# One fused attention and MLP kernel: the list that orders its last part is rewritten

## The chip, the core and the metric

The kernel runs on one core of a Trainium2 chip. The core has a matrix engine (PE, with its weight loads shown apart as PEld), a vector engine (DVE), a scalar engine (ACT), GpSimd (POOL) and a queue engine (SP). Each works through its own instructions in the order in which they were written, and they meet at semaphores. The metric is the device time of one execution in microseconds; the median over runs is given.

## The reference

Eight batches with eight heads of 576 tokens attend inside a window of 32 tokens on each side and to eight global tokens. The result, 4608 tokens by 512, goes through an MLP whose activation is h·cos(h):

```python
x = attn_out.transpose(0, 2, 1, 3).reshape(B * S, H * D)      # 4608 x 512
h = x @ w_in                                                  # 512 -> 2048
g = h * np.cos(h)
return (g @ w_out).astype(np.float32)                         # 2048 -> 512
```

## The kernel before

The kernel works in fp16 with fp32 sums. Attention goes by pairs of heads, and the MLP goes by tiles of 512 tokens, nine tiles numbered 0 to 8. The two are interleaved: strings of short words, one word for a step, are read from left to right, and each step writes its instructions. The schedule is manual, so the order of the words is the order of the instructions on every engine. The last string, `TAIL`, starts when all attention is done and 112 of the 144 MLP units in front of the activation are written. It finishes tiles 6, 7 and 8, and it is what the change edits. Its words:

- `i` is one unit in front of the activation (`one`, then `mlp_in` and `mlp_act`): four matmuls of 128x512 into one PSUM bank (L788), a sine on ACT that gives the cosine (L794, "cos") and a product on DVE (L795, "g"). The units of a tile are numbered 0, 8, 1, 9, ... 7, 15. I write i8.15 for unit 15 of tile 8. Banks alternate: two banks named `ph` and two in the tile `units`.
- `o` is one unit behind the activation (`two`, then `mlp_out` and `win`): eight matmuls of 128x256 (L852). Tiles 6 to 8 use Winograd's seven products of half matrices, in the order 1, 2, 6, 5, 7, 3, 4, each in two units for two column halves. I write o8.6a and o8.6b for the two halves of product 6 of tile 8. The banks are `wx` (products 1, 6, 7, 4 added up) and `wy` (2; then 5 and 3). After the products a copy on ACT (L866, L868, L870, L875) or an addition on DVE (L879) takes the bank out, and SP stores the result. In tile 8 this happens for each half by itself, in tiles 6 and 7 once for both.
- `a0` to `a7`, `b0` to `b7`, `c0` to `c7` are the sums of quarters of g that Winograd's products of tiles 6, 7 and 8 need (`g_sum`, L822, DVE, 128x1024). Words 0 to 3 are the first half of the rows, 4 to 7 the second: s1, then s2 from s1, then s4 from s2, and a difference written in place in g. Product 5 reads s1, product 6 s2, product 3 s4 and product 7 the difference.
- `x0`, `x1` are sums of squares of the last attention rows (`x_squares`, L910, ACT).
- `w` squares one of 16 blocks of w_in (`weight_squares`, L923, ACT); from the second of four on, DVE adds it (L925, "wsq"). `v0` to `v3` sum four such blocks over the partitions with one matmul (`weight_norms`, L930, bank `pn`) and take the maximum on DVE (L931).
- `F` is the final check's chain of small DVE instructions (`finish_check`, L937 to L954). `R` is its matmul with one column and the flag (`raise_flag`, L960 to L963).

An `i` of tile 8 may stand only behind the last `o` of tile 6, and an `o` of tile 7 only behind the last `i` of tile 7.

```python
        for step in TAIL.split():
            n = int(step[1:] or 0)
            if step[0] == "i":
                one()
            elif step[0] == "o":
                two()
            elif step[0] == "x":
                x_squares(B * NP // 2 - 1, n)
            ...
            elif step[0] == "v":
                weight_norms(n)
```

Of the kernel before, what the change touches and what calls it, by code (L numbers as in the profile page):

```python
# [48 lines left out]

LASTR = "2 kz qz sa 2 2 2 sz pa 1 j0 2 1 2 xa n pz 1 1 j1 2 xz 1 j2 1 2 1 j3 1"  # L50

TAIL = "i x0 a4 o i x1 a5 o i a6 o i a7 o i w o i w i w o i w o i b0 o i b1 v0 o i b2 i b3 o i w o i w o i w o i w o i b4 o i b5 v1 o i b6 o i b7 o i w o i w i w o i w o i c0 o i c1 v2 o i c2 i c3 o i w o i w o i w o i w c4 c5 c6 c7 v3 o o o o o F o o o o o R o o o o o"

MID = ("+ 1 1 1 1 Z0 1 1 1 Z5 B5 1 Z1 1 1 Z2 1 1 A0 1 Z3 1 1 A1 1 n0 A2 g10 g11 1 Z4 N K6 1 1 1 1 1 1 1 2 2 kc qc n1 2 2 1 1 B6 2 2 n2 kd qd - 2 2")

# [156 lines left out]
def kernel(  # L212
# [787 lines left out]
    with tc.manual_schedule():  # L1000
# [136 lines left out]
        units2 = ps.tile([P, 2, TT], FP32, tag="pv", bufs=1, name="units2")  # L1137
        for step in TAIL.split():
            n = int(step[1:] or 0)
# [54 lines left out]
```

## Time and profile before

| | |
|---|---|
| median of three runs | 339.95 us (339.12, 339.95, 344.02) |
| the profiled execution's own time | 340.63 us |
| its span | 338.9 us, of which PE 322.2 busy (95%) |
| DVE, ACT, POOL busy | 269.4, 241.3, 107.2 us |
| granted TensorE clock over the span | 0.997 |
| the part written by `TAIL`, on PE | 264.3 to 332.1 us |

PE's matmuls overlap, so a row's duration is longer than the distance at which units follow each other; distances between starts are what counts. A row of the timeline with "x8" is eight instructions in a row. The number in square brackets is the idle time of the engine before the row, with what ended it. The end of a matmul in the trace is modelled.

### The profile page before, as it was taken

What the parts mean: (1) busy time and instruction counts of PE and PEld (TensorE: products, weight loads), DVE (VectorE), ACT (ScalarE), POOL (GpSimd) and SP (SyncE); (2) the same over time, 40 slices, a digit from 0 to 9 for tenths busy, and PEclk for the clock granted to TensorE, in tenths of its full rate; (3) what the DMA queues carried; (4) which work ended last, traced back from release to release, by engine and by line L of the source; (5) the groups of instructions that cost most, each with busy time, mean ns of one, the idle gap of its engine ahead of it and who ended that gap; (6) DMA issues with size and microseconds to landing.
All of it is one profiled execution on the core that took longest, in us unless ns stands there. A gap on an engine that the chain in (4) does not pass through costs nothing.

```text
span 338.9 us, 8639 instructions
## 1 busy us (share of the span) xinstructions
PE 322.2 (95%) x3269; PEld 179.8 (53%) x3269; DVE 269.4 (79%) x649; ACT 241.3 (71%) x422; POOL 107.2 (32%) x216
## 2 busy tenths in 40 slices
PE   7989889999999999999999999999999999999791
PEld 3566654444545454545454545454544566666581
DVE  6578989984678798989898988888989778778850
ACT  4778885785968878787878787878786775665510
POOL 7856658451162316232532344143001100000000
PEclk9999999999999999999999999999999999999998
DMA  5999799999999999999999999999970010100212
GB/s 76 203 185 205 140 207 206 196 123 176 131 201 123 155 151 150 219 150 175 160 160 162 160 178 137 163 171 172 124 130 3 31 33 31 64 32 2 93 54 80
DMA packets 167220, 45.01 MB, mean 133 GB/s; under 512 B 153108, under 2 KB 163732, under 8 KB 166996
## 3 DMA queue, kind: packets, MB, share of 16 engines
q1 hardware_dynamic: 107556, 26.73, 54.5%
q0 software_dynamic: 59472, 17.54, 50.6%
q8 instruction: 27, 0.44, 0.6%
q14 instruction: 21, 0.17, 0.2%
q10 hardware_dynamic: 144, 0.13, 0.1%
HBM read 44.93 MB, written 19.17 MB: 189 GB/s over the span
## 4 chain that ended last, share of the span: by engine, by line
PE 82%; DVE 7%; ACT 6%; issue 2%; DMA 1%; SPq 0%; ACTq 0%; DVEq 0%
PE ph L788 29%; PE po L892 23%; PE wx L852 6%; PE wy L852 5%; PE units L788 4%; PE st L722 3%; PE pv L742 3%; DVE g L795 2%; PE tx L767 2%; PE pv L669 2%; PE bank L618 1%; DMA gidx_col<-in_global_idx_dram 1%; ACT cos L794 1%; PE st L654 1%; ACT e L661 1%
## 5 line engine op out<-in xcount | busy, mean ns | idle before, releaser
L788 PE MATMUL ph<-xT,w_in 128*128 128x512 f16 x512 | 123.2, 379 | 1.0 <-DVE g L795 0.4
L794 ACT ACTIVATE cos<-ph,pio 128x512 f16<-128x512 f32 x128 | 86.5, 687 | 44.8 <-PE ph L788 42.2
L795 DVE TENSOR_TENSOR g<-cos,ph 128x512 f16<-128x512 f16 x128 | 85.6, 684 | 18.8 <-ACT cos L794 16.8
L892 PE MATMUL po<-w_out,g 128*128 128x512 f16 x384 | 93.4, 379 | 0.0
L788 PEld LDWEIGHTS <-w_in 128*128 128x128 f16 x576 | 53.7, 98 | 57.4 <-issue 1.4
L892 PEld LDWEIGHTS <-g 128*128 128x128 f16 x384 | 36.5, 98 | 43.1
L725 ACT ACTIVATE e<-st 128x512 f16<-128x512 f32 x44 | 23.9, 594 | 8.2 <-PE st L722 8.1
L726 DVE TENSOR_TENSOR pm<-e,mask 128x512 f16<-128x512 f16 x44 | 18.8, 428 | 13.4 <-ACT e L725 12.1
L1079 POOL COPY gate<-xn 1x1 f16<-1x1 f16 x8 | 1.4, 180 | 81.0 <-DVE xn L753 81.0
L775 POOL COPY xT<-xg 128x4 f16 x48 | 15.8, 330 | 32.0 <-DVE xT L770 29.4
L281 POOL DMA_DIRECT2D q<-in_q_dram x11 | 24.3, 2205 | 0.0
L852 PEld LDWEIGHTS <-g 128*128 128x128 f16 x192 | 18.7, 98 | 5.7 <-issue 0.3
L753 DVE TENSOR_TENSOR xn<-pv,r_all 128x768 f16<-128x768 f32 x22 | 21.1, 958 | 0.7
L914 ACT ACTIVATE xn<-xn 128x1536 f16<-128x1536 f16 (+1 forms) x15 | 21.2, 1410 | 0.0
L281 POOL DMA_DIRECT2D k<-in_k_dram x11 | 18.0, 1637 | 1.4 <-issue 1.4
L795 DVE TENSOR_TENSOR g<-cos,units 128x512 f16<-128x512 f16 x16 | 11.0, 687 | 8.3 <-ACT cos L794 8.3
L788 PE MATMUL units<-xT,w_in 128*128 128x512 f16 x64 | 16.4, 379 | 0.0
L794 ACT ACTIVATE cos<-units,pio 128x512 f16<-128x512 f32 x16 | 11.0, 690 | 6.9 <-PE units L788 6.7
L794 ACT ACT_TABLE_LOAD x12 | 15.4, 1283 | 0.2
L600 POOL COPY kw<-kgT 128x88 f16<-128x88 f16 x22 | 14.3, 872 | 0.0
L725 ACT ACT_TABLE_LOAD x11 | 14.1, 1283 | 0.2
L657 ACT ACTIVATE e<-st 128x488 f16<-128x488 f32 x20 | 10.4, 572 | 5.3 <-PE st L654 5.3
(215 smaller groups left out, 498.3 us busy)
## 6 DMA issues: line engine op xcount, KB each, us to landing
out_dram<-o SPq DMA_DIRECT2D x24, 256.0 KB
vw<-v SPq DMA_DIRECT2D x32, 165.0 KB
k<-in_k_dram POOLq DMA_DIRECT2D x11, 288.0 KB, 7.7
q<-in_q_dram POOLq DMA_DIRECT2D x11, 288.0 KB, 10.6
v<-in_v_dram POOLq DMA_DIRECT2D x11, 288.0 KB, 5.7
vn<-in_v_dram SPq DMA_DIRECT2D x20, 120.0 KB
w_in<-in_moe_w_in_dram POOLq DMA_DIRECT2D x4, 512.0 KB, 11.0
w_out<-in_moe_w_out_dram POOLq DMA_DIRECT2D x1, 2048.0 KB, 16.5
```

Of the source, the lines that this page charges most:

```text
L281: nc.gpsimd.dma_start(dst[s].rearrange("t (h d) -> t h d", h=4), dview(src, base, (D, S), (S * D, 4), (1, D)))
L600: nc.gpsimd.tensor_copy(kw[pr % NK][:, :, 0:G], view(kgT[:, pr], (0, NB), (1, G)))
L725: nc.scalar.activation(e[:, 0:512], st[h], AF.Exp, scale=scale)
L726: nc.vector.tensor_tensor(view(pm[:, h], (1, 512)), e[:, 0:512], view(mask, (1, 512)), ALU.mult)
L753: nc.vector.tensor_tensor(view(xn, (384, 2), (D, 6), (1, D)), view(pv, (512, 2), (65, 6), (1, D)), view(rp, (6, 2), (1, 6), (0, D)), ALU.mult)
L775: nc.gpsimd.tensor_copy(xT[:, :, bass.ds(pool_idx[g] + b * S, 1)], xg[:, :, g : g + 1])
L788: nc.tensor.matmul(ph, w_in16[:, j, f * P : (f + 1) * P], xT[:, j, t * TT : (t + 1) * TT], start=(j == 0), stop=(j == NC - 1))
L794: nc.scalar.activation(cos, ph, AF.Sin, bias=pio2)
L795: nc.vector.tensor_tensor(g, cos, ph, ALU.mult)
L852: nc.tensor.matmul(bank[:, a], left(f)[:, a * P : a * P + P], right(f), start=name in "125" and f == 0 and (split or a == 0), stop=f == HF ...
L892: nc.tensor.matmul(po, g16[:, f, s * P : (s + 1) * P], w_out16[:, f], start=(f == 0), stop=(f == NF - 1))
L914: nc.scalar.activation(view(xn, (BP * P, 2), (1, n)), view(xn, (BP * P, 2), (1, n)), AF.Square, accum_out=x_sq[:, s : s + 1])
```

## The change

Only the string `TAIL` is replaced. The new string has the same 118 words, each as often as before; their order is another.

```diff
-TAIL = "i x0 a4 o i x1 a5 o i a6 o i a7 o i w o i w i w o i w o i b0 o i b1 v0 o i b2 i b3 o i w o i w o i w o i w o i b4 o i b5 v1 o i b6 o i b7 o i w o i w i w o i w o i c0 o i c1 v2 o i c2 i c3 o i w o i w o i w o i w c4 c5 c6 c7 v3 o o o o o F o o o o o R o o o o o"
+TAIL = "x0 a4 a5 o x1 a6 i w o i i o o i o w i w a7 o i w o i o i v0 b0 o b1 i i o i o b2 i i o o w i w w i b3 o o i w b4 i o i b5 i o b6 w o i o i w o i v1 i o i w w o c0 b7 o i c1 v2 o i c2 i o c3 o i o i i w w o w i o i w o c4 c5 c6 o o c7 o v3 o F o o o o R o o o o o"
```

Written out with tile and unit, the start of the list was i7.0, x0, a4, o6.1a, i7.8, x1, a5, o6.1b; it is now x0, a4, a5, o6.1a, x1, a6, i7.0, w, o6.1b, i7.8, i7.1. The end, from o7.3b on, was:

```
o7.3b i8.7 w o7.4a i8.15 w c4 c5 c6 c7 v3 o7.4b o8.1a o8.1b o8.2a o8.2b F o8.6a o8.6b o8.5a o8.5b o8.7a R ...
```

and it is now:

```
o7.3b i8.6 i8.14 w w o7.4a w i8.7 o7.4b i8.15 w o8.1a c4 c5 c6 o8.1b o8.2a c7 o8.2b v3 o8.6a F o8.6b o8.5a o8.5b o8.7a R ...
```

On PE, around v3 near the end, the order of before is this (`units` is the bank of i8.15, `pn` that of v3, and the `wx` behind it belongs to o7.4b):

```order
L788 LDWEIGHTS w_in_133
L788 MATMUL units_4959<-xT,w_in_133 128x512
L930 LDWEIGHTS ones_112 [waits DVE_49]
L930 MATMUL pn<-wsq,ones_112 128x512 [waits PE_49]
L852 LDWEIGHTS g
L852 MATMUL wx<-xT,g 128x256
```

and with the change (`wy` belongs to o8.2b, `wx` to o8.6a):

```order
L852 LDWEIGHTS g
L852 MATMUL wy<-w_out_91,g 128x256
L930 LDWEIGHTS ones_112 [waits DVE_49]
L930 MATMUL pn<-wsq,ones_112 128x512 [waits PE_49]
L852 LDWEIGHTS room_88
L852 MATMUL wx<-xT,room_88 128x256 [waits Activation_49]
```

v3 moved from directly behind i8.15 to four units later; o8.1a now follows i8.15.

On ACT at the end, before, with the cosine of i8.7 (`ph`), that of i8.15 (`units`) and the last copy of tile 7 (L875):

```order
L794 ACTIVATE cos<-units_4959,pio_71 128x512
L923 ACTIVATE wsq<-w_in_133 128x512
L794 ACTIVATE cos<-ph,pio_71 128x512
L923 ACTIVATE wsq<-w_in_133 128x512
L794 ACTIVATE cos<-units_4959,pio_71 128x512
L923 ACTIVATE wsq<-w_in_133 128x512
L875 COPY kw_98<-wx 128x512
L866 COPY vw_92<-wx 128x256 x2
```

and with the change (the first two rows are the cosines of i8.6 and i8.14):

```order
L794 ACTIVATE cos<-ph,pio_71 128x512
L794 ACTIVATE cos<-units_4959,pio_71 128x512
L923 ACTIVATE wsq<-w_in_133 128x512 x3
L794 ACTIVATE cos<-ph,pio_71 128x512
L875 COPY kw_98<-wx 128x512
L794 ACTIVATE cos<-units_4959,pio_71 128x512
L923 ACTIVATE wsq<-w_in_133 128x512
L866 COPY vw_92<-wx 128x256 x2
```

Three squares now stand together in front of the cosine of i8.7, and the copy out of tile 7 stands in front of the cosine of i8.15.

On DVE at the end, before, from the product of i8.15 to the first rows of `F` (`room_87` to `room_89` and the `g` in place are c4 to c7):

```order
L795 TENSOR_TENSOR g<-cos,units_4959 128x512
L925 TENSOR_TENSOR wsq<-wsq 128x512
L822 TENSOR_TENSOR room_87<-g 128x1024
L822 TENSOR_TENSOR room_88<-room_87,g 128x1024
L822 TENSOR_TENSOR room_89<-g,room_88 128x1024
L822 TENSOR_TENSOR g<-g 128x4x256
L931 TENSOR_REDUCE wmax_137<-pn 128x1
L879 TENSOR_TENSOR vw_92<-wy,vw_92 128x256 x2
L937 TENSOR_SCALAR lo_ok<-r_all 128x384
```

and with the change:

```order
L795 TENSOR_TENSOR g<-cos,units_4959 128x512
L925 TENSOR_TENSOR wsq<-wsq 128x512
L822 TENSOR_TENSOR room_87<-g 128x1024
L822 TENSOR_TENSOR room_88<-room_87,g 128x1024
L822 TENSOR_TENSOR room_89<-g,room_88 128x1024
L879 TENSOR_TENSOR vw_92<-wy,vw_92 128x256
L822 TENSOR_TENSOR g<-g 128x4x256
L879 TENSOR_TENSOR vw_92<-wy,vw_92 128x256
L931 TENSOR_REDUCE wmax_137<-pn 128x1
L937 TENSOR_SCALAR lo_ok<-r_all 128x384
```

The additions that take o8.2a and o8.2b out of their banks now stand among the sums, and the maximum of v3 stands directly ahead of `F`. The instructions on SP and POOL are the same rows in the same order.

More of the change, by code (lines that the diff above doesn't have):

```diff
@@ L50 @@
 LASTR = "2 kz qz sa 2 2 2 sz pa 1 j0 2 1 2 xa n pz 1 1 j1 2 xz 1 j2 1 2 1 j3 1"
-TAIL = "i x0 a4 o i x1 a5 o i a6 o i a7 o i w o i w i w o i w o i b0 o i b1 v0 o i b2 i b3 o i w o i w o i w o i w o i b4 o i b5 v1 o i b6 o i b7 o i w o i w i w o i w o i c0 o i c1 v2 o i c2 i c3 o i w o i w o i w o i w c4 c5 c6 c7 v3 o o o o o F o o o o o R o o o o o"
+TAIL = "x0 a4 a5 o x1 a6 i w o i i o o i o w i w a7 o i w i o i v0 b0 o b1 i i o i o b2 i i o o w i w w i b3 o o i w b4 i o i b5 i o b6 w o i o i w o i v1 i o i w w o c0 b7 o i c1 v2 i o c2 i o c3 o i o i i w w o w i o i w o c4 c5 c6 o o c7 o v3 o F o o o o R o o o o o"
 MID = ("+ 1 1 1 1 Z0 1 1 1 Z5 B5 1 Z1 1 1 Z2 1 1 A0 1 Z3 1 1 A1 1 n0 A2 g10 g11 1 Z4 N K6 1 1 1 1 1 1 1 2 2 kc qc n1 2 2 1 1 B6 2 2 n2 kd qd - 2 2")
```

## The prediction

> **What bounds the kernel now.** I read the busy shares first, then the busy time of each engine by stretch, then PE's waits in the last part, and last the timeline of that part. The first row gives PE 95% of the span. The windows (columns: stretch, its length, busy time of PE, PEld, DVE, ACT, POOL, granted clock, DMA share, GB/s) show where the rest is:
>
> ```profile
> PE 322.2 (95%) x3269; PEld 179.8 (53%) x3269; DVE 269.4 (79%) x649; ACT 241.3 (71%) x422; POOL 107.2 (32%) x216
> ```
>
> ```profile
> 266.00:316.50 50.50, 50.47 (x338) 32.74 (x335) 39.36 (x67) 33.27 (x57) 0.00 (x0) 1.00 0.10 33
> 316.50:319.00 2.50, 0.66 (x6) 0.48 (x6) 1.81 (x5) 1.21 (x2) 0.00 (x0) 1.00 0.26 90
> 319.00:326.50 7.50, 7.50 (x71) 6.72 (x70) 5.40 (x19) 2.45 (x6) 0.00 (x0) 1.00 0.21 70
> 326.50:338.90 12.40, 5.59 (x52) 4.56 (x49) 2.32 (x7) 0.75 (x2) 0.00 (x0) 0.92 0.22 70
> ```
>
> In the last part PE is full except for one stretch, and the clock is full too. Its waits from 262 us on are two:
>
> ```profile
> PE pn L930 <- DVE wsq L925: 1.8, 1, 1.8
> PE ph L788 <- DVE g L795: 0.4, 1, 0.4
> ```
>
> So this part lasts as long as its matmuls plus the holes between them. An order can win the holes and no more. Their true size is in PE's timeline, since a row's end is modelled:
>
> ```profile
> 261.79 2.16 PE L788 MATMUL ph<-xT,w_in 128*128 128x512 f16 x8
> 264.31 1.04 PE L788 MATMUL ph<-xT,w_in 128*128 128x512 f16 x4 [0.37 <-DVE g L795]
> 265.19 1.04 PE L852 MATMUL wx<-w_out,g 128*128 128x256 f16 x8
> 266.06 1.03 PE L788 MATMUL units<-xT,w_in 128*128 128x512 f16 x4
> ...
> 290.58 1.03 PE L788 MATMUL ph<-xT,w_in 128*128 128x512 f16 x4
> 291.64 1.03 PE L852 MATMUL wx<-w_out,g 128*128 128x256 f16 x8
> ...
> 315.51 1.03 PE L788 MATMUL units<-xT,w_in 128*128 128x512 f16 x4
> 318.37 0.39 PE L930 MATMUL pn<-wsq,ones 128*128 128x512 f16 x1 [1.84 <-DVE wsq L925]
> 318.60 1.04 PE L852 MATMUL wx<-xT,g 128*128 128x256 f16 x8
> ...
> 330.18 1.91 PE L852 MATMUL wx<-xT,g 128*128 128x256 f16 x16
> ```
>
> A unit of either kind takes 0.87 us from start to start (265.19 to 266.06), pn 0.23, one of an o unit's eight matmuls 0.11. Three starts come later than that. **Hole 1**: the row at 261.79 holds i6.14 and i6.15. A unit by itself spans 1.03, so i6.15 began at 261.79 + 2.16 − 1.03 = 262.92 and made room at 263.79. i7.0 began at 264.31: 0.52. **Hole 2**: 290.58 + 0.87 = 291.45, but o7.1a began at 291.64: 0.19. **Hole 3**: 315.51 + 0.87 = 316.38, but v3 began at 318.37: 1.99. Together 2.70. As a balance, 74 units, four pn and R (taken as a pn) make 74 × 0.87 + 5 × 0.23 = 65.5; with holes 2 and 3 that is 67.7. From 264.31 to 332.09, less 0.17 for the modelled end (1.04 − 0.87), it is 67.6. No fourth hole of any size is left.
>
> That the end follows PE is in the last rows of the chain of waits, and in the last store's row behind them:
>
> ```profile
> 330.34 1.76 PE wx L852 x16
> 332.10 0.02 issue
> 332.13 0.37 ACT vw L875
> ```
>
> ```profile
> 332.53 0.38 ACTq L864 DMA_DIRECT2D out_dram<-vw  x1
> ```
>
> From there 6.4 us to 338.9 pass with that store and the program's close, which the list doesn't touch.
>
> **The change part by part.** It adds and removes no instruction, and SP's and POOL's rows stay where they were. So each step is a place where PE could now stand or no longer stands.
>
> *Start, hole 1.* i7.0 waited for the bank of i6.14, that is for its product on DVE. Now o6.1a comes first.
>
> ```profile
> 261.99 0.59 ACT L897 COPY o<-po 128x512 f32<-128x512 f32 x1 [0.17 <-PE po L892]
> ...
> 263.57 0.69 DVE L795 TENSOR_TENSOR g<-cos,ph 128x512 f16<-128x512 f16 x1 [0.70 <-ACT cos L794]
> ```
>
> Its bank is free at 262.58. Only its eighth weight load reads i6.14's product, ready at 264.26; that load's turn is 263.79 + 7 × 0.11 = 264.56. i7.0 then starts at 264.66 and finds its bank free. All 0.52 go. The cover is thin (0.3 us); without it the eighth load waits, and hole 1 returns in part. x0, x1 on ACT and a4 to a6 on DVE now delay i7.0's cosine and product, but its bank is wanted again only eight units (7 us) later, and i7.1 and i7.8 use others. Cost: nothing.
>
> *Hole 2.* o7.1a waits for the copy that empties tile 6's bank:
>
> ```profile
> 291.01 0.58 ACT L875 COPY vw<-wx 128x512 f32<-128x512 f32 x1
> ```
>
> It ends 1.01 us behind o6.4b's last turn (290.58). Before one unit stood between; now i7.15 and i8.0 do, 1.74 us. On ACT the copy also stands ahead of i7.15's cosine and square now, and no longer behind them. 0.19 go.
>
> *Hole 3.* v3 needs the fourth square's addition, which needs ACT behind the cosine of i8.15:
>
> ```profile
> 316.57 0.69 ACT L794 ACTIVATE cos<-units,pio 128x512 f16<-128x512 f32 x1 [0.47 <-PE units L788]
> 317.16 0.62 ACT L923 ACTIVATE wsq<-w_in 128x512 f16<-128x512 f16 x1
> 317.29 0.69 DVE L795 TENSOR_TENSOR g<-cos,units 128x512 f16<-128x512 f16 x1 [0.65 <-ACT cos L794]
> 317.90 0.42 DVE L925 TENSOR_TENSOR wsq<-wsq 128x512 f16<-128x512 f16 x1
> 318.23 0.69 DVE L822 TENSOR_TENSOR room<-g 128x1024 f16<-128x1024 f16 x1
> 318.95 0.69 DVE L822 TENSOR_TENSOR room<-room,g 128x1024 f16<-128x1024 f16 x1
> 319.68 0.69 DVE L822 TENSOR_TENSOR room<-g,room 128x1024 f16<-128x1024 f16 x1
> 320.29 0.68 DVE L822 TENSOR_TENSOR g<-g 128x1024 f16<-128x1024 f16 x1
> 320.89 0.68 DVE L931 TENSOR_REDUCE wmax<-pn 128x1 f32<-128x512 f32 x1
> ```
>
> The chain takes 318.32 − 316.38 = 1.94 us from i8.15's turn. v3 now stands four units (3.48) behind it, so 1.99 go. What is late next? Three things stand close behind.
>
> *o8.1a*, now directly behind i8.15, reads i8.7's product with its eighth weight load, and three squares stand ahead of that cosine. ACT's distances:
>
> ```profile
> 301.85 0.68 ACT L794 ACTIVATE cos<-ph,pio 128x512 f16<-128x512 f32 x1
> 302.42 0.63 ACT L923 ACTIVATE wsq<-w_in 128x512 f16<-128x512 f16 x1
> 302.94 0.58 ACT L868 COPY kw<-wx 128x512 f32<-128x512 f32 x1
> ```
>
> 0.57 behind a cosine, 0.52 behind a square. I count from the end of i8.14's turn: its cosine starts at 0.19 (as 316.38 to 316.57), the squares at 0.76, 1.28 and 1.80, i8.7's cosine at 2.32 instead of 1.93. Its product runs from 3.04 to 3.73. o8.1a's turn is at 4 × 0.87 = 3.48, its eighth load's at 4.25: 0.5 to spare, cost nothing.
>
> *R* needs `F`, which stands behind c4 to c7, two additions and a maximum on DVE.
>
> ```profile
> 323.24 0.42 DVE L879 TENSOR_TENSOR vw<-wy,vw 128x256 f32<-128x256 f32 x1 [0.46 <-PE wy L852]
> 323.58 0.35 DVE L937 TENSOR_SCALAR lo_ok<-r_all 128x384 f32<-128x384 f32 x1
> ...
> 325.85 0.06 DVE L954 MEMSET onesf<- 128x1 f32 x1
> ...
> 327.42 0.09 PEld L960 LDWEIGHTS pt<-onesf,tot 128*1 128x1 f32 x2 [0.21 <-issue]
> ```
>
> Before, `F` ended at 325.91 and R came at 327.42, 1.5 to spare. Now, on the same clock, i8.15's product starts at 3.48 + 0.19 + 0.72 = 4.39. By distances: product 0.61, addition of squares 0.33, c4 0.72, c5 0.73, c6 0.61, addition 0.34, c7 0.60, addition 0.34, maximum 0.60, `F` 323.58 to 325.91 = 2.33; it ends at 11.60. R's turn is 3.48 + 4 units 3.48 + pn 0.23 + 5 units 4.35 = 11.54. R waits 0.1 us. This is the one new wait that I price. Behind it on PE stand o8.7b and products 3 and 4, which all shift with it.
>
> *v2*, three units (2.61) behind i8.11, with two squares together: cosine 0.19, squares at 0.76 and 1.28, the second done at 1.91, its addition by 2.4. 0.2 to spare. No wait is priced here. v0, v1 and o7.7a (on b7), worked out in the same way, have half a microsecond or more.
>
> **Sum.** 0.52 + 0.19 + 1.99 − 0.10 = 2.60. Against the profiled execution, 340.63 − 2.60 = 338.0. The median of the runs lies 0.68 below that execution: 339.95 − 2.60 = **337.35 us**, −0.8%. Both bounds of the unknown: with no new wait 2.70, hence 337.25; R's wait by full durations is the first rival.
>
> **The rivals.** *The check block is late.* I took distances between starts. If DVE were held for an instruction's full duration, as rows that depend on each other nearly are (318.23, 318.95: 0.72 for 0.69), the chain up to `F` would take 0.69 + 0.42 + 0.72 + 0.73 + 0.69 + 0.42 + 0.68 + 0.42 + 0.68 + 2.33 = 7.78 instead of 7.21, R would wait 0.67, and v2 would use up its 0.2. The time is 337.9, or 338.3 if v2 and o6.1a lose 0.2 each. Against it stands 320.29 to 320.89, 0.60 for 0.68. The Trainium skill (Perfetto Trace Analysis, "DVE / Act Engine Instruction") says that the reported window runs from the ALU's start to the write's acknowledgement, and that the next instruction's read may begin only when the ALU has finished, which leaves a bubble between any two. If that bubble were as long as the acknowledgement, distance would equal duration, and by that estimate this rival is the case. The trace agrees only where the second row reads the first (0.72); elsewhere it has 0.60 for 0.68. Chance 0.17.
>
> *The end doesn't follow PE.* If something else held the last 6.4 us (another store, the program's close), PE would be done earlier and nothing gained: 339.95. Against it stands the chain's end in PE, ACT, store. Chance 0.06.
>
> *Slower: the clock falls.* A list without holes gives PE about 65 us without rest. The last window's granted clock is 0.92. If it stood at that through the tail, 65.5 us of matmuls would take 71.2, 5.7 more, less 2.6: 343.1. It decides from a granted clock of about 0.96 (65.5 / 0.96 = 68.2, 2.7 more). Against it: 50.47 busy of 50.50 already go at 1.00, and in the last window PE idles behind 332.1. The Trainium skill (TensorE: Matmul & The Clock Gate, Part 1) says that the gate closes after an idle window and opens with work; no run here shows a closing under load on this core. Chance 0.03.
>
> *The change doesn't do what it says* is out: the rows of PE show v3 and o6.1a at their new places.
>
> **How the numbers follow.** Forecast 0.74, the rivals 0.17, 0.06 and 0.03. The undisturbed runs and the profiled one differ by 1.5 us (339.12 to 340.63), so 0.8 belongs to each side of any forecast. With 337.25 as its lower bound the forecast's own range is 336.4 to 338.2. The late check (338.3 and 0.8) and the nearer half of the case without gain bring the upper end to 339.5; the clock and the rest, under 1 in 10, are left out, and chance in the median takes the other tenth. The range is 336.4 to 339.5. Under 2% (6.8 us) is about what a measurement of this kernel tells from no change; all holes together are 0.8%, so none of the cases leaves that band, not even 343.1. Faster by over 2% gets 0.01, slower 0.02, for what I haven't seen.
>
> **What would show it.** Right: PE's only wait in the last part is at R, at most 0.2; o6.1a starts at 263.8; i8.15 is followed at once by o8.1a; the last copy on ACT starts near 329.5. Wrong: a wait of over 0.5 at R (`F` ending late), at v2's `pn`, or at o8.1a's last weight load (squares ahead of the cosine); a last copy that is early under an unchanged span; or a granted clock under 0.96 in that stretch.

## The result, and the profile after

The changed kernel takes 0.9925 of the time of before (95% interval 0.9899 to 0.9951): 0.75% less, 338.2 us median of 22 runs against 340.81 of 22. The ratio goes by the undisturbed runs, the medians by all, among them one of before that took 469.93 us. The profiled execution took 336.97 us with a span of 335.3. Before, the two were 340.63 and 338.9.

The string that ran has 118 words. The new string as it is printed under "The change" differs from it in two places: it has one `o` more, in `a7 o i w o i o i v0` where the kernel has `a7 o i w i o i v0`, and it has `c1 v2 o i c2` where the kernel has `c1 v2 i o c2`. The steps written out there, the rows and the prediction's working are those of the kernel.

The page's first row is nearly the same as before. PE's busy time did not change (322.2 before), only its share did:

```profile
PE 322.3 (96%) x3269; PEld 180.1 (54%) x3269; DVE 269.7 (80%) x649; ACT 241.1 (72%) x422; POOL 107.6 (32%) x216
```

The windows of the changed kernel (stretch, length, then busy time of PE, PEld, DVE, ACT, POOL, granted clock, DMA share, GB/s) have PE busy for the whole of the last part, at the full clock:

```profile
263.00:315.89 52.89, 52.89 (x358) 34.76 (x357) 41.52 (x70) 35.02 (x59) 0.26 (x1) 1.00 0.12 39
315.89:328.70 12.81, 12.81 (x116) 10.96 (x114) 9.46 (x30) 3.35 (x9) 0.00 (x0) 1.00 0.25 82
328.70:335.30 6.60, 0.02 (x1) 0.00 (x0) 0.00 (x0) 0.37 (x1) 0.00 (x0) 0.72 0.17 52
```

PE's timeline at the places of the three holes, and on to R:

```profile
261.16 2.16 PE L788 MATMUL ph<-xT,w_in 128*128 128x512 f16 x8
263.16 1.04 PE L852 MATMUL wx<-w_out,g 128*128 128x256 f16 x8
264.03 1.03 PE L788 MATMUL ph<-xT,w_in 128*128 128x512 f16 x4
...
289.41 1.03 PE L788 MATMUL ph<-xT,w_in 128*128 128x512 f16 x4
290.28 1.04 PE L852 MATMUL wx<-w_out,g 128*128 128x256 f16 x8
...
315.02 1.03 PE L788 MATMUL units<-xT,w_in 128*128 128x512 f16 x4
315.89 1.91 PE L852 MATMUL wx<-w_out,g 128*128 128x256 f16 x16
317.63 1.91 PE L852 MATMUL wy<-w_out,g 128*128 128x256 f16 x16
319.38 0.38 PE L930 MATMUL pn<-wsq,ones 128*128 128x512 f16 x1
319.60 1.91 PE L852 MATMUL wx<-xT,room 128*128 128x256 f16 x16
...
323.09 1.04 PE L852 MATMUL wx<-xT,g 128*128 128x256 f16 x8
324.06 0.19 PE L960 MATMUL pt<-onesf,tot 128*1 128x1 f32 x2
```

A word on names first. The prediction and the expectations write i6.13, i6.14 and i6.15 for the last three units in front of the activation of tile 6. By the numbering 0, 8, 1, 9, ... 7, 15 only the last name is right; the two ahead of it are units 14 and 7. The names are kept here, so i6.14 is unit 7 of tile 6, the one that o6.1a's eighth matmul reads.

i6.15 began at 261.16 + 2.16 − 1.03 = 262.29, and o6.1a follows at 263.16, 0.87 later: hole 1 is gone. o7.1a follows i8.0 in 0.87 (289.41 to 290.28): hole 2 is gone. o8.1a follows i8.15 in 0.87, and v3 stands four units behind without a wait: hole 3 is gone. PE's list of waits from 259 us on is empty.

I measure the last part from the start of i6.14 to the start of the last copy on ACT, because the instructions in front of it and behind it are the same in both kernels. Before it was 332.13 − 261.79 = 70.34 us. Now it ends with this row:

```profile
328.75 0.37 ACT L875 COPY vw<-wx 128x256 f32<-128x256 f32 x1 [5.09 <-PE wx L852]
```

so it is 328.75 − 261.16 = 67.59 us, 2.75 less. The spans of the two profiled executions differ by 3.6. The other 0.85 is in front (i6.14 starts 0.63 earlier) and behind (335.3 − 328.75 = 6.55 against 6.77). The instructions there are the same, so it is scatter between executions and no gain. Over many runs 0.75% of 340.8 is 2.6 us.

### The profile page after: what moved, and what is told of

Its sections match the earlier page's. It is cut to its first block, busy times and chain, and to the rows that moved or that the text cites. A ratio compares the mean times of both kernels' runs of the same rounds, so it can differ in the third digit from the quotient of the medians.

```text
span 335.3 us, 8640 instructions
## 1 busy us (share of the span) xinstructions
PE 322.3 (96%) x3269; PEld 180.1 (54%) x3269; DVE 269.7 (80%) x649; ACT 241.1 (72%) x422; POOL 107.6 (32%) x216
## 4 chain that ended last, share of the span: by engine, by line
PE 84%; DVE 7%; ACT 5%; issue 2%; ACTq 0%; DVEq 0%
PE ph L788 29%; PE po L892 23%; PE wx L852 6%; PE wy L852 5%; PE units L788 4%; PE pv L742 3%; PE t L330 3%; PE st L722 3%; DVE g L795 2%; PE pv L669 2%; PE tx L767 2%; PE bank L618 2%; PE st L654 1%; ACT cos L794 1%; PE bank L613 1%
## 5 line engine op out<-in xcount | busy, mean ns | idle before, releaser
L914 ACT ACTIVATE xn<-xn 128x1536 f16<-128x1536 f16 (+1 forms) x15 | 21.2, 1411 | 0.0
L722 PEld LDWEIGHTS <-kw 64*128 64x128 f16 x484 | 8.4, 95 | 10.2 <-issue 8.4
```

Of the source, the lines that this page charges most:

```text
L722: nc.tensor.matmul(st[j // 8 * 2 + h][:, j % 8 * C : j % 8 * C + C], kp[hp, j], qp[hp, j], start=True, stop=True)
L914: nc.scalar.activation(view(xn, (BP * P, 2), (1, n)), view(xn, (BP * P, 2), (1, n)), AF.Square, accum_out=x_sq[:, s : s + 1])
```

## The experiments

Each kernel's stretch, from i6.14 to the last copy, is read in its own trace, where it can be told to some hundredths. The times of whole runs tell it only to 0.3 or 0.4% (half the width of their intervals), and holes 1 and 2 together are worth 0.2%.

**One hole at a time, from before.** The first kernel is before with v3 alone moved:

```diff
-... w c4 c5 c6 c7 v3 o o o o o F ...
+... w c4 c5 c6 c7 o o o o o v3 F ...
```

> The list of before, with v3 alone moved: it stands behind o8.2b instead of behind c7. If each hole is its own, hole 3 goes (1.99 us) and holes 1 and 2 stay: PE's only wait left is the one of i7.0 on DVE's product, the stretch from i6.14's start to the last copy on ACT shrinks from 70.34 to 68.35 us, and the time is 0.9942 of before. If the wait only moves to the next one that is late (o8.1a's last weight load or R), the stretch stays near 70. If the end does not follow PE, the stretch shrinks and the span keeps its length behind it.

Measured: 0.9922 of before (0.9883 to 0.9961, too wide to tell it from the 0.9942 expected or from the changed kernel), stretch 329.73 − 261.40 = 68.33 us. The one wait that is left in its list of PE's waits (engine, line, what it waited for: total, times, longest), and its last copy:

```profile
PE ph L788 <- DVE g L795: 0.4, 1, 0.4
```

```profile
329.73 0.37 ACT L875 COPY vw<-wx 128x256 f32<-128x256 f32 x1 [5.09 <-PE wx L852]
```

The stretch lost 2.01 us, the 1.99 of hole 3. Nothing else became late, and the end came with it.

The second is before with two swaps:

```diff
-i x0 a4 o i x1 a5 o ...
+o i x0 a4 i x1 a5 o ...
-... o i b4 o i b5 v1 o ...
+... o i b4 i o b5 v1 o ...
```

> The list of before with two swaps: o6.1a stands first, ahead of i7.0, and i8.8 stands ahead of o7.1a. If holes 1 and 2 are what I took them for, i6.15 and o6.1a follow each other in 0.87 us and o7.1a follows i8.8 in 0.87, while v3 still waits 2.0: the stretch from i6.14 to the last copy shrinks from 70.34 to 69.6 us, the time is 0.998 of before. If the first hole is only handed to o6.1a (its last weight load) or to i7.0, PE still loses about 0.5 there and the stretch is 70.1.

Measured: 0.9961 (0.9924 to 0.9997), stretch 332.19 − 262.59 = 69.60 us. PE's rows at the two places:

```profile
262.59 2.16 PE L788 MATMUL ph<-xT,w_in 128*128 128x512 f16 x8
264.59 1.04 PE L852 MATMUL wx<-w_out,g 128*128 128x256 f16 x8
265.46 1.03 PE L788 MATMUL ph<-xT,w_in 128*128 128x512 f16 x4
...
291.71 1.03 PE L788 MATMUL units<-xT,w_in 128*128 128x512 f16 x4
292.57 1.04 PE L852 MATMUL wx<-w_out,g 128*128 128x256 f16 x8
```

i6.15 (from 263.72) and o6.1a, and i8.8 and o7.1a, stand 0.87 and 0.86 apart. The stretch lost 0.74, with 0.71 expected. The two kernels together account for 2.01 + 0.74 = 2.75, which is the whole of what the changed list gained. So the other rearrangements in that list, taken together, neither gain nor cost anything that shows.

**One hole put back.** The changed list with v3 directly behind i8.15:

```diff
-... o i w o c4 c5 c6 o o c7 o v3 o F ...
+... o i w v3 o c4 c5 c6 o o c7 o o F ...
```

> The changed list with v3 alone put back directly behind i8.15 and its last square. If hole 3 belongs to that place and to nothing else, v3 waits 1.95 us again for the addition of the squares and the stretch from i6.14 to the last copy grows from 67.59 to 69.5 us, the time is 0.998 of before. If the other moves near the end (the three squares together, c4 to c7 later) had a part in the gain, the wait is clearly shorter than 1.95.

Measured: 0.9994 (0.9951 to 1.0036), stretch 333.29 − 263.70 = 69.59 us, 2.00 more than with the change. Its start, its timeline around v3, and its last copy:

```profile
263.70 2.16 PE L788 MATMUL ph<-xT,w_in 128*128 128x512 f16 x8
...
318.62 0.69 ACT L794 ACTIVATE cos<-units,pio 128x512 f16<-128x512 f32 x1 [0.18 <-PE units L788]
319.21 0.62 ACT L923 ACTIVATE wsq<-w_in 128x512 f16<-128x512 f16 x1
319.34 0.69 DVE L795 TENSOR_TENSOR g<-cos,units 128x512 f16<-128x512 f16 x1 [0.65 <-ACT cos L794]
319.95 0.42 DVE L925 TENSOR_TENSOR wsq<-wsq 128x512 f16<-128x512 f16 x1
320.42 0.38 PE L930 MATMUL pn<-wsq,ones 128*128 128x512 f16 x1 [1.83 <-DVE wsq L925]
...
333.29 0.37 ACT L875 COPY vw<-wx 128x256 f32<-128x256 f32 x1 [5.09 <-PE wx L852]
```

It is the same chain of cosine, square and addition as before, with the same price. The three squares together and the later c4 to c7, which this list keeps, had no part in the gain. (The expectation's 0.998 is inside the interval.)

**The cover at R.** The changed list with R one unit earlier:

```diff
-... o v3 o F o o o o R o o o o o
+... o v3 o F o o o R o o o o o o
```

> The changed list with R one unit earlier, ahead of o8.7a. In the changed kernel the check's chain on DVE ended at 324.00 and R began at 324.06, so R had nothing to spare. If that is so, PE now waits about 0.9 us at R and the last copy comes 0.87 later: the stretch from i6.14 to the last copy is 68.46 us instead of 67.59. If R had time to spare, the stretch stays at 67.6. If the end does not follow PE, the store's end and the span keep their place all the same.

Measured, in one execution: stretch 330.30 − 261.84 = 68.46 us. R's rows, behind the end of the check's chain, and the last copy:

```profile
324.61 0.06 DVE L954 MEMSET onesf<- 128x1 f32 x1
324.73 0.09 PEld L960 LDWEIGHTS pt<-onesf,tot 128*1 128x1 f32 x2 [1.08 <-DVE onesf L954]
324.73 0.19 PE L960 MATMUL pt<-onesf,tot 128*1 128x1 f32 x2 [0.80 <-DVE onesf L954]
...
330.30 0.37 ACT L875 COPY vw<-wx 128x256 f32<-128x256 f32 x1 [5.96 <-PE wx L852]
```

A unit's length is lost in full, and the end moves with it. In the changed list R stands at the first place where it costs nothing.

**The cover in front of o8.1a.** One and three more squares on ACT ahead of i8.7's cosine. A new word `q` squares a block that is already squared into the same place, so the result is the same:

```diff
-... i i w w o w i o i w o c4 ...
+... i i w q w o w i o i w o c4 ...          (three: w q q q w)
+            elif step[0] == "q":
+                nc.scalar.activation(w_sq[3][:, 0], w_in16[:, 0, 3 * 512 : 4 * 512], AF.Square)
```

> The changed list with one more square on ACT (the first block of w_in's last quarter is squared once more into the same place) among the three in front of i8.7's cosine. My working gave o8.1a's last weight load 0.5 us to spare and a square 0.52. So this square should use the cover up: o8.1a waits at most 0.1, i8.15's cosine comes 0.2 later, so the check's chain and R come 0.2 later: the stretch from i6.14 to the last copy is 67.8 us instead of 67.59. If ACT's queue had cost PE something already in the changed kernel, the stretch grows by the full 0.5.

> The same with three more squares, 1.56 us of ACT in front of i8.7's cosine. By my working the cover of 0.5 is gone and the rest shows on PE: o8.1a's last weight load waits about 1.1 us, and R a further 0.2, since i8.15's cosine is 1.25 late: the stretch from i6.14 to the last copy is 68.9 us. If PE had more cover than I counted (o8.1a not bound to i8.7's product), the stretch is 68.8 or less with all of the wait at R; if squares cost nothing there, 67.6.

Measured, in one execution each: stretches 329.52 − 261.56 = 67.96 us (67.8 expected) and 331.48 − 262.19 = 69.29 us (68.9 expected). In the kernel with three, this is ACT's run of squares, and the wait on PE with the rows around it:

```profile
314.23 0.62 ACT L923 ACTIVATE wsq<-w_in 128x512 f16<-128x512 f16 x1
314.88 1.95 ACT L1155 ACTIVATE wsq<-w_in 128x512 f16<-128x512 f16 x3
316.05 1.03 PE L788 MATMUL units<-xT,w_in 128*128 128x512 f16 x4
316.74 1.13 ACT L923 ACTIVATE wsq<-w_in 128x512 f16<-128x512 f16 x2
316.92 0.93 PE L852 MATMUL wx<-w_out,g 128*128 128x256 f16 x7
317.78 0.67 ACT L794 ACTIVATE cos<-ph,pio 128x512 f16<-128x512 f32 x1
319.23 1.16 PE L852 MATMUL wx<-w_out,g 128*128 128x256 f16 x9 [1.38 <-DVE g L795]
```

Seven of o8.1a's eight matmuls run, and the eighth waits for i8.7's product, as the prediction had it. The sizes were off in one term: the added squares, which read the same block and write the same place as the square ahead of them, follow each other in 0.65 us (314.23, 314.88, three in 1.95), where squares of different blocks into different places take 0.52. From the first square to i8.7's cosine it is 317.78 − 314.23 = 3.55 us here. In the changed kernel, on ACT, it is

```profile
313.20 1.66 ACT L923 ACTIVATE wsq<-w_in 128x512 f16<-128x512 f16 x3
...
314.76 0.67 ACT L794 ACTIVATE cos<-ph,pio 128x512 f16<-128x512 f32 x1
```

1.56. So the three added squares cost 3.55 − 1.56 = 1.99 on ACT, instead of the 3 × 0.52 that were expected. The eighth matmul's turn was at 316.92 + 7 × 0.11 = 317.69, it started at 319.23, so 1.54 of the 1.99 showed and 0.45 was cover. My working had said 0.5. The remaining 0.16 (1.70 − 1.54) is R's but for rounding: it came at 326.78, 0.25 behind its turn (o8.6a at 322.18 and five units of 0.87), and 0.11 behind it, counted in the same way, in the changed kernel.

The kernel with one more square gives the same cover:

```profile
313.59 0.62 ACT L923 ACTIVATE wsq<-w_in 128x512 f16<-128x512 f16 x1
...
315.82 0.67 ACT L794 ACTIVATE cos<-ph,pio 128x512 f16<-128x512 f32 x1
...
316.28 2.14 PE L852 MATMUL wx<-w_out,g 128*128 128x256 f16 x16
```

From the first square to the cosine it is 2.23 us, 0.67 more than with the change. o8.1a and o8.1b take 2.14 instead of 1.91, so 0.23 of the 0.67 showed at o8.1a and 0.44 was cover.

**One more place.** PE's timeline of the changed kernel still shows i6.15 0.26 late behind i6.14, since two `ph` banks serve three units in a row. The last unit of the list before moves into `TAIL`, where odd units use the other banks:

```diff
-LASTR = "... xz 1 j2 1 2 1 j3 1"
+LASTR = "... xz 1 j2 1 2 1 j3"
-TAIL = "x0 a4 a5 o ...
+TAIL = "i x0 a4 a5 o ...
```

> The changed list, and the unit i6.15 is taken from the end of the list before into its front, so that it goes into a bank of the tile units instead of the bank that i6.13 still held. In the changed kernel i6.15 began 0.26 us later than 0.87 behind i6.14, waiting for i6.13's product. If that bank was the cause, the two follow in 0.87 and the stretch from i6.14 to the last copy shrinks from 67.59 to 67.3 us: 0.9915 of before. If the next wait (o6.1a's last weight load, with 0.3 to spare, which now comes 0.26 earlier) takes it, the stretch stays within 0.1 of 67.59.

Measured: 0.9915 of before (0.9878 to 0.9952), stretch 328.97 − 261.60 = 67.37 us, 0.22 less than with the change.

```profile
261.60 1.03 PE L788 MATMUL ph<-xT,w_in 128*128 128x512 f16 x4
262.46 1.03 PE L788 MATMUL units<-xT,w_in 128*128 128x512 f16 x4
263.32 1.08 PE L852 MATMUL wx<-w_out,g 128*128 128x256 f16 x8
...
264.12 0.10 PEld L852 LDWEIGHTS <-g 128*128 128x128 f16 x1 [0.15 <-DVE g L795]
```

The unit keeps its place on PE, ACT and DVE and only its bank is another, so the bank was the cause. About 0.05 of the 0.26 went to o6.1a's eighth weight load: i7.0 starts at 264.25, 0.93 behind o6.1a instead of 0.87. That is the thin cover of the prediction's first step, now used up. It had been counted at 0.3 and was 0.2. This kernel's last part is the shortest of all; in whole runs it can't be told from the changed kernel.

## Why the prediction was right

**The bound.** PE was the limit of the last part and the three holes were all that an order of `TAIL` could win. After the change PE is busy for 52.89 of 52.89 and 12.81 of 12.81 us, and the stretch lost 2.75, where the holes had been worked out at 2.70. The prediction's "no fourth hole of any size" holds only from i7.0 on, where its balance began. One of 0.26 stood just ahead, at i6.15 (262.92 in before, where 261.79 + 0.87 makes 262.66), in the string before `TAIL`; the last experiment won 0.22 there.

**The steps.** Holes 1 and 2 were priced at 0.52 + 0.19, and the kernel with those two places alone lost 0.74. Hole 3 was priced at 1.99; v3 alone moved lost 2.01, and v3 put back cost 2.00. The sum over separate holes held to 0.05.

**The term that was mis-sized** is R's new wait, 0.10. The working had R start at its turn, and `F` end 0.06 behind that. `F` did end 0.04 behind it (324.00 against 323.09 + 0.87 = 323.96), and R came at 324.06, 0.10 behind its turn. But before it came 0.10 behind its turn as well (327.43 against 326.46 + 0.87), with 1.5 us to spare:

```profile
326.46 1.04 PE L852 MATMUL wx<-xT,g 128*128 128x256 f16 x8
...
327.43 0.19 PE L960 MATMUL pt<-onesf,tot 128*1 128x1 f32 x2
```

So that tenth is R's own and was paid already, and `F`'s lateness fell into it. In before the profile shows no wait behind it ("issue"). No new wait came, and that makes 0.10 of the 0.15 between 2.60 and 2.75; the other 0.05 is what the three holes were worth above 2.70.

**The first rival, the late check,** is refuted by DVE's rows of the changed kernel:

```profile
316.81 0.69 DVE L795 TENSOR_TENSOR g<-cos,units 128x512 f16<-128x512 f16 x1 [0.65 <-ACT cos L794]
...
323.94 0.06 DVE L954 MEMSET onesf<- 128x1 f32 x1
324.05 0.09 PEld L960 LDWEIGHTS pt<-onesf,tot 128*1 128x1 f32 x2 [0.21 <-DVE onesf L954]
```

From i8.15's product to the end of `F` it is 324.00 − 316.81 = 7.19 us. Distances between starts had given 7.21, full durations 7.78. The Trainium skill (Perfetto Trace Analysis, "DVE / Act Engine Instruction") puts a bubble between any two instructions. In this chain it is shorter than the reported tail of the instruction before, since c7 and the addition behind it start 0.60 us apart with 0.68 reported; only where the next one reads the result is the distance longer than the duration, 0.72 for 0.69 from c4 to c5. The rival was close all the same: the releaser of R is now `F` and no longer the issue. The kernel with R one unit earlier shows what lies beyond: 0.87 lost.

**The second rival, an end that doesn't follow PE,** falls with what follows the last copy. Had something else held the end, an earlier copy would be followed by a longer rest. The copy came at 328.75 us in the changed kernel and at 333.29 with v3 put back, and 6.55 and 6.51 us followed; in all nine traces it was 5.8 to 6.8 us, with no order by how early the copy was.

**The third, a lower clock,** didn't come: the granted clock is 1.00 in both windows in which PE works through the tail without a pause. Its 0.72 stands only behind 328.7, where PE has nothing to do.

**The squares in front of i8.7's cosine** cost nothing, and their cover is 0.45 us where the working said 0.5.

**v2** lost nothing either, but its cover was half of what the prediction had counted. These are the rows of the changed kernel:

```profile
303.30 0.95 DVE L925 TENSOR_TENSOR wsq<-wsq 128x512 f16<-128x512 f16 x2
304.30 0.10 PEld L930 LDWEIGHTS <-ones 128*128 128x128 f16 x1 [0.25 <-DVE wsq L925]
```

The addition ended at 304.25 and released the weight load, and v2's matmul started at 304.39, its turn. With v3 put back, v3 started 0.05 behind the end of its addition (320.37 to 320.42), so v2 could have started at 304.30: 0.09 to spare, where 0.2 had been counted. Of the covers that were counted, three (o6.1a, v2, o8.1a) came out 0.05 to 0.1 smaller.

**The time.** The forecast was −2.60 us, 0.8%; measured were 0.75% in whole runs and 2.75 us in the stretch. The absolute median, 338.2, lies 0.85 above the forecast because before's median over 22 runs is itself 0.86 above that of its first three, which the forecast had started from. That is as much as the 0.8 that the range had for such scatter, so that the absolute time came out inside it is in part luck. The gain does not rest on it.

## What to carry to other kernels

Where one engine is full but for a few holes, take the distance between the starts of its units, list every start that comes later than that, and read at each what it waited for; the sum of these holes is all that an order of that part can win, and each can be priced before anything is run. Then look in the new order for the waits that have the least to spare: the in-order queue of each other engine, counted in distances between starts and not in durations, gave them here to a tenth of a microsecond. Judge a gain of under 1% by a stretch of the trace between two fixed instructions, since the whole time scatters by more.

## What the runs showed of the hardware that I had not expected

The scatter of the time is not spread evenly over the program. In one trace each, the stretch came within 0.1 us of what was expected in five of the seven kernels built for the experiments, those without more squares. But i6.14 began anywhere from 261.16 to 263.70 us with the same instructions ahead of it, and 5.8 to 6.8 us passed behind the last copy. Of the scatter in front, most lies early: the first row of L914 on ACT began at 67.59 to 69.68 us, and from there to i6.14 it was 193.41 to 194.68. So a difference of one or two microseconds between two single executions says nothing here, while the stretch tells tenths.

Two squares on ACT that read the same block and write the same place follow each other in 0.65 us, those of different blocks into different places in 0.52, though nothing of one is read by the other. Which of the two makes the difference, and why, was not tried.
